# A gated attention and long-convolution kernel on one core: 24 places of its stored task order changed, and its last tenth put in a new order

## The chip, the cores and the metric

The kernel runs on one core of a Trainium2 chip. The core has five engines with a queue of instructions each: TensorE (PE in the profile; its weight loads are listed apart as PEld), VectorE (DVE), ScalarE (ACT), GpSimd (POOL) and SyncE (SP), and 16 DMA engines that they share. The metric is the device time of one execution in microseconds; the median of several runs is compared.

## The reference

B = 8 batches, S = 3136 positions, D = 256 channels, 64 channels for the scores; everything comes in and goes out in f32.

```python
scores = np.matmul(z, z.transpose(0, 2, 1)) / S
attn = np.maximum(scores, 0.0) ** 2
x = u * np.matmul(attn, v)
proj = x @ w_proj                      # 256 -> 768
x1, x2, x3 = proj[..., :D], proj[..., D:2*D], proj[..., 2*D:]
X2 = np.fft.rfft(x2, n=S, axis=1)
H = np.fft.rfft(filter_fft, n=S, axis=0)[None]
conv = np.fft.irfft(X2 * H, n=S, axis=1)
out = (x1 * conv * x3) @ w_out
```

The scores are symmetric, since both sides are z.

## The kernel before, in words

**The stages of a batch.** The 3136 positions of a batch are cut into seven chunks (five of 512, one of 256, one of 320). Attention goes by units, pairs of 128-row tiles against a chunk: PE multiplies z with z into a PSUM pair, ACT or DVE takes the relu of it (L1956 on ACT, L1958 on DVE, into a tile R_t of which there are 3), ACT or DVE squares it (L1965, L1967, into A_t, of which there are 8), and PE weighs v with it. Because the scores are symmetric, a squared tile also serves the mirrored unit, after a DMA transpose on SP's queue (L1885, into M_t, M2e_t or M2o_t by chunk). DVE multiplies the sum with u into xT_t (L2012). For a chunk PE then makes the projection; ACT or DVE evicts one gate factor (x_t), DVE makes the gate product (gate_t, L1293).

**The convolution** is an FFT of 3136 = 64 x 49 written as matmuls with two round trips over DRAM. The first transform is evicted to s_t and put to DRAM (L1065, L1068), and loaded back with the other index on the partitions (L1099; for the last batch L1114, into spec_in_t and gs_t). PE transforms again ("quads"), evicts to xh and R_t (L619, ACT's copies; L623, DVE's), DVE multiplies with the filter's spectrum (L1394, L1398, L1399), PE transforms back, the result is evicted (in the last batch into M_t, M2e_t, M2o_t, A_t and uT_t, which are free by then), put to DRAM (L1443) and loaded again (L1128, into conv_in_t, v_t or A_t). PE makes the last step, DVE multiplies with the gate into yT_t (L1499), PE applies w_out, ACT or DVE evicts (ost_t; for the last batches also v_t, R_t, xh, gs_t) and the rows are stored (L1548).

**Who loads and stores.** POOL issues the loads of u, v and z (L662, L688) behind small copies that wait for a task (L673, L676), and casts z and v at the start. SP issues mirrors, the turns of z and u (L1657, L1602), puts, loads and most stores, strictly in its own order: an instruction that waits holds up those behind it. In the last 50 us some ends of batches 5 and 6 are left over for PE to work on during the last batch's round trips, and batch 6's stores go by POOL's queue.

**What sets the order.** All this is some 5,400 tasks. A class Plan holds them with the engines that each may run on and what each waits for. Its function go walks four tables at the head of the file. ORDER (L50) names the tasks two characters at a time, for all engines in one sequence, in which each engine's instructions are issued; ENGINES (L163) says for each task that could go to either ACT ("a") or DVE ("d") which one takes it; BANKS (L180) names the PSUM pair for each task of PE that takes one; CODES is the alphabet. An entry of ORDER past the last task is a filler: eight matmul instructions with an identity that no one reads (in the profile ps_s<-ident). The times the class works with are its own; nothing but these tables decides the order.

Of the kernel before, what the change touches and what calls it, by code (L numbers as in the profile page):

```python
# [2106 lines left out]
```

## Time and profile before

| | |
|---|---|
| runs | 941.12, 946.83, 946.80 us; median 946.8 |
| the profiled execution | 942.77 us, of which its span 940.9; granted clock 0.997 |
| PE, DVE, ACT, POOL busy | 914.0, 838.7, 819.6, 247.6 us |
| matmuls | 12425 |
| DMA moved | 170.70 MB, mean 181 GB/s |
| the chain that ended last | 83% of it on PE, 5% each on ACT, DVE and DMA |

The page gives busy times and, further down, groups of instructions by source line. A row of a timeline has the start in us, the length, the engine, the line, the operation with its tiles and how many, and in brackets how long the engine was idle before and what it is thought to have waited for. A row of the chain of waits has start, length and the engine with the tile. A row of the windows has, for a stretch of time, the busy time of PE, weight loads, DVE, ACT and POOL with the number of instructions, then PE's granted clock, the busy share of the DMA engines and the GB/s they moved. Several instructions of one kind in a row stand in one row.

### The profile page before, as it was taken

What the parts mean: (1) busy time and instruction counts of PE and PEld (TensorE: products, weight loads), DVE (VectorE), ACT (ScalarE), POOL (GpSimd) and SP (SyncE); (2) the same over time, 40 slices, a digit from 0 to 9 for tenths busy, and PEclk for the clock granted to TensorE, in tenths of its full rate; (3) what the DMA queues carried; (4) which work ended last, traced back from release to release, by engine and by line L of the source; (5) the groups of instructions that cost most, each with busy time, mean ns of one, the idle gap of its engine ahead of it and who ended that gap; (6) DMA issues with size and microseconds to landing.
All of it is one profiled execution on the core that took longest, in us unless ns stands there. A gap on an engine that the chain in (4) does not pass through costs nothing.

```text
span 940.9 us, 30306 instructions
## 1 busy us (share of the span) xinstructions
PE 914.0 (97%) x12425; PEld 555.4 (59%) x12425; DVE 838.7 (89%) x1117; ACT 819.6 (87%) x952; POOL 247.6 (26%) x585
## 2 busy tenths in 40 slices
PE   8999999999999999999999999999999999999985
PEld 3445655566554666556565565666565666676654
DVE  8886899999888998999889988999988999899795
ACT  7877898999889998898989999899988999899673
POOL 5143322332332312223122231333123141101030
PEclk9999999999999999999999999999999999999999
DMA  9899899989999789998999989998999979898867
GB/s 158 155 176 163 141 156 197 185 144 173 169 218 201 151 190 168 206 200 146 192 173 212 177 160 189 178 223 149 200 167 208 224 128 202 202 205 140 207 193 232
DMA packets 331644, 170.70 MB, mean 181 GB/s; under 512 B 242887, under 2 KB 307143, under 8 KB 331505
## 3 DMA queue, kind: packets, MB, share of 16 engines
q1 hardware_dynamic: 301624, 131.98, 70.2%
q0 software_dynamic: 29168, 35.13, 25.8%
q8 instruction: 97, 1.59, 0.7%
q10 hardware_dynamic: 712, 1.66, 0.6%
q14 instruction: 43, 0.34, 0.2%
HBM read 90.26 MB, written 53.05 MB: 152 GB/s over the span
## 4 chain that ended last, share of the span: by engine, by line
PE 83%; ACT 5%; DMA 5%; DVE 5%; issue 2%; SPq 0%; POOL 0%; DVEq 0%; ACTq 0%; POOLq 0%
PE ps_s L553 82%; DMA M_t<-A_t 3%; ACT R_t L1956 2%; DVE xh L1394 1%; DVE A_t L1967 1%; DMA zn_t<-in_z_dram 1%; ACT A_t L1965 1%; DVE xT_t L2012 1%; DMA A_t<-spec 0%; ACT xh L619 0%; DMA spec<-uT_t 0%; ACT ost_t L619 0%; ACT s_t L619 0%; DVE gs_t L623 0%; ACT R_t L619 0%
## 5 line engine op out<-in xcount | busy, mean ns | idle before, releaser
L553 PE MATMUL ps_s<-A_t,v_t 64*128 64x512 bf16 (+5 forms) x4766 | 515.7, 352 | 1.1 <-DVE A_t L1967 1.0
L553 PEld LDWEIGHTS <-v_t 64*128 64x128 bf16 (+1 forms) x6528 | 305.8, 98 | 185.9 <-PE ps_s L553 19.2
L1956 ACT ACTIVATE R_t<-ps_s 128x1024 f32<-128x1024 f32 (+3 forms) x359 | 336.8, 961 | 50.4 <-PE ps_s L553 47.2
L1965 ACT ACTIVATE A_t<-R_t 128x1024 bf16<-128x1024 f32 (+2 forms) x281 | 271.8, 992 | 12.0 <-DVE R_t L1958 4.9
L1967 DVE SCALAR_TENSOR_TENSOR A_t<-R_t 128x1024 bf16<-128x1024 f32 (+3 forms) x211 | 233.6, 1123 | 17.6 <-ACT R_t L1956 10.3
L553 PE MATMUL ps_s<-zT_t 64*128 64x512 bf16 (+5 forms) x1186 | 191.4, 352 | 4.4 <-DVE gate_t L1293 1.7
L1958 DVE TENSOR_SCALAR R_t<-ps_s 128x1024 f32<-128x1024 f32 (+4 forms) x153 | 170.3, 1124 | 23.7 <-PE ps_s L553 13.3
L676 POOL COPY tick<-A_t 1x1 bf16<-1x1 bf16 x159 | 54.3, 341 | 426.0 <-ACT A_t L1965 262.0
L553 PE MATMUL ps_s<-xT_t,wp 64*128 64x512 bf16 (+3 forms) x976 | 124.3, 352 | 0.5 <-DVE R_t L1958 0.4
L553 PEld LDWEIGHTS <-zT_t 64*128 64x128 bf16 (+1 forms) x1219 | 68.9, 97 | 52.8 <-issue 9.8
L553 PE MATMUL ps_s<-M_t,v_t 64*128 64x512 bf16 (+4 forms) x860 | 96.6, 353 | 1.8 <-DMA M_t<-A_t 1.7
L619 ACT ACTIVATE x_t<-ps_s 128x1024 bf16<-128x1024 f32 (+3 forms) x75 | 69.4, 927 | 20.9 <-PE ps_s L553 18.1
L1394 DVE TENSOR_TENSOR xh<-xh,H 128x1024 bf16<-128x1024 bf16 x120 | 81.8, 685 | 2.9 <-ACT xh L619 2.0
L1293 DVE TENSOR_TENSOR gate_t<-ps_s,x_t 128x512 bf16<-128x512 f32 (+2 forms) x112 | 64.5, 617 | 12.4 <-PE ps_s L553 10.3
L2012 DVE TENSOR_TENSOR xT_t<-ps_s,uT_t 128x512 bf16<-128x512 f32 (+2 forms) x112 | 64.0, 614 | 6.5 <-PE ps_s L553 6.1
L1499 DVE TENSOR_TENSOR yT_t<-ps_s,gate_t 128x1024 bf16<-128x1024 f32 (+2 forms) x53 | 56.9, 1078 | 12.9 <-PE ps_s L553 11.7
L553 PEld LDWEIGHTS <-wp 64*128 64x128 bf16 (+1 forms) x976 | 47.8, 96 | 30.0 <-PE ps_s L553 2.0
L553 PE MATMUL ps_s<-wp,xT_t 64*128 64x256 bf16 (+2 forms) x944 | 64.0, 266 | 0.1
L553 PE MATMUL ps_s<-wo,yT_t 64*128 64x256 bf16 (+2 forms) x904 | 62.3, 266 | 1.0 <-DVE yT_t L1499 0.5
L662 POOL DMA_DIRECT2D un_t<-in_u_dram x112 | 58.1, 519 | 18.5 <-issue 16.0
L688 POOL DMA_DIRECT2D v_t<-in_v_dram x112 | 58.4, 525 | 13.6 <-issue 10.3
L553 PEld LDWEIGHTS <-xT_t 64*128 64x128 bf16 (+1 forms) x944 | 43.5, 97 | 19.1 <-issue 0.6
(157 smaller groups left out, 910.2 us busy)
## 6 DMA issues: line engine op xcount, KB each, us to landing
out_dram<-ost_t SPq DMA_DIRECT2D x60, 256.0 KB
spec_in_t<-spec SPq DMA_DIRECT2D x56, 192.0 KB
spec<-gs_t SPq DMA_DIRECT2D x56, 192.0 KB
v_t<-in_v_dram POOLq DMA_DIRECT2D x80, 128.0 KB, 4.5
un_t<-in_u_dram POOLq DMA_DIRECT2D x80, 128.0 KB, 4.5
spec<-s_t SPq DMA_DIRECT2D x40, 256.0 KB
conv_in_t<-spec SPq DMA_DIRECT2D x34, 256.0 KB
out_dram<-ost_t SPq DMA_DIRECT2D x18, 128.0 KB
```

The source lines that it names most:

```text
L553: got = nc.tensor.matmul(o, *args, **kw)
L619: got = nc.scalar.activation(out_, in_, AF.Copy)
L662: nc.gpsimd.dma_start(out=t[ds(j * N1, N1), lo - t0 : hi - t0, :], in_=x[:, n2 : n2 + hi - lo, :])
L688: nc.gpsimd.dma_start(out=t[ds(j * N1, N1), ds(v_at(a), (b - a) * D)], in_=r[:, n2 + a - lo : n2 + b - lo, :].rearrange("p t d -> p (t d)"),)
L1293: has_read(nc.vector.tensor_tensor(o[:, :, ::-1] if h == 0 else o, p, x, ALU.mult), p)
L1394: nc.vector.tensor_tensor(x[:, 1 - i], x[:, 0], h, ALU.mult)
L1499: has_read(nc.vector.tensor_tensor(yb["y"][:, :, 0:w], p, gates[b, c][:, :, 0:w], ALU.mult), p)
L1956: has_read(nc.scalar.activation(r, p, AF.Relu), p)
L1958: has_read(nc.vector.tensor_single_scalar(r, p, 0.0, ALU.max), p)
L1965: nc.scalar.activation(a, r, AF.Square, scale=1.0 / float(S))
L1967: nc.vector.scalar_tensor_tensor(a, r, inv_s2, r, ALU.mult, ALU.mult)
L2012: has_read(nc.vector.tensor_tensor(x[:, :, ::-1] if h == 0 else x, f, ut, ALU.mult), f)
```

## The change

Only the tables change; the tasks and what they compute are the same. ORDER had 13 fillers and has 7. Some 30 tasks change between ACT and DVE, three of them before 850 us: one relu of the first batch goes from DVE to ACT, and two squares. ACT has 955 activations instead of 951. Named by the times of the profile before, the places up to 850 us are:

- 29: a relu moves to ACT and PE takes its neighbours in another order; 64 to 72: POOL's casts ahead of a filter load; 66 to 71, 85, 91, 119: PE swaps neighbouring matmuls
- 164: SP's turn of u later; 270 to 311: SP's mirrors earlier, stores and a spectrum put later
- 375: a square on ACT one place earlier; 393 (to 409) a store later, 484 a turn of u later, 541 (to 552) and 618 (to 628) stores later, all on SP
- 491, 599, 618: PE swaps neighbours; 607: a square to ACT; 839 to 850: a turn of u and a square on ACT earlier

From about 852 us on the whole of the rest is new. The diff is three long tables; its first line that differs, and one of ENGINES:

```diff
 ORDER = (
...
-    "1S1P1a1c110M1Xr!1d1U1g0N1b1Er#1h1k1Y1er$1l1o1J1ir%1f1p1m1s1j1=1tr&1qr(1>1]1n1u1}1^22r)231r1?1v271_r*"
+    "1S1P1a1c110M1Xr!1d1U1g1E0N1br#1h1k1Y1er$1l1o1ir%1f1J1p1m1s1j1=1tr&1qr(1>1]1n1u1}1^22r)231r1?1v271_r*"
...
 ENGINES = (
...
-    "aaaaaaaadaaaaaadaaaadadaad"
+    "aaaaaadadaadaaadaaaadaddad"
```

**SP, around 270 to 291 us.** SP's queue; the rows are mirrors (M2e_t, M2o_t, M_t, out of A_t), turns of z and u, spectrum loads and output stores (out_dram). Before:

```order
L1099 DMA spec_in_t<-spec_1_60 48x2048 x2
L1099 DMA spec_in_t<-spec_1_60 2x2048
L1885 DMA_TRANSPOSE M2e_t<-A_t 128x8x128
L1657 DMA_TRANSPOSE zT_t<-zd_t 128x8x128
L1602 DMA_TRANSPOSE uT_t<-un_t 128x8x128
L1548 DMA out_dram<-ost_t 64x1024 x4
L1099 DMA spec_in_t<-spec_1_60 48x2048 x2
L1099 DMA spec_in_t<-spec_1_60 2x2048
L1885 DMA_TRANSPOSE M2o_t<-A_t 128x8x128
L1885 DMA_TRANSPOSE M_t<-A_t 128x8x128 x2
L1443 DMA spec_1_62<-gs_t 48x2048 x2
```

Now:

```order
L1885 DMA_TRANSPOSE M2e_t<-A_t 128x8x128
L1099 DMA spec_in_t<-spec_1_60 48x2048 x2
L1099 DMA spec_in_t<-spec_1_60 2x2048
L1657 DMA_TRANSPOSE zT_t<-zd_t 128x8x128
L1602 DMA_TRANSPOSE uT_t<-un_t 128x8x128
L1548 DMA out_dram<-ost_t 64x1024 x2
L1099 DMA spec_in_t<-spec_1_60 48x2048 x2
L1099 DMA spec_in_t<-spec_1_60 2x2048
L1885 DMA_TRANSPOSE M2o_t<-A_t 128x8x128
L1885 DMA_TRANSPOSE M_t<-A_t 128x8x128 x2
L1548 DMA out_dram<-ost_t 64x1024 x2
```

The M2e_t mirror is now ahead of a load, and two of the four stores stand behind the M2o_t and M_t mirrors.

**POOL, the end of its queue.** v_t, ost_t, R_t and xh hold finished rows; ost_t and v_t are batch 6's, R_t and xh the last batch's. Before:

```order
L1443 DMA spec_1_62<-A_t 2x1024
L1443 DMA spec_1_62<-uT_t 2x1024
L1548 DMA out_dram<-v_t 64x512 x2
L1548 DMA out_dram<-v_t 64x768
L1548 DMA out_dram<-v_t 64x512
L1548 DMA out_dram<-ost_t 64x1024 x2
L1548 DMA out_dram<-R_t 64x1024
L1548 DMA out_dram<-xh_118 64x1024
```

Now:

```order
L1443 DMA spec_1_62<-uT_t 2x1024
L1548 DMA out_dram<-v_t 64x1024 x2
L1548 DMA out_dram<-v_t 64x512 x2
L1548 DMA out_dram<-R_t 64x1024
L1548 DMA out_dram<-ost_t 64x1024 x2
L1548 DMA out_dram<-xh_118 64x1024
L1548 DMA out_dram<-v_t 64x768
L1548 DMA out_dram<-v_t 64x512
L1548 DMA out_dram<-ost_t 64x1024 x2
```

Three of batch 6's stores (ost_t twice, the 64x768 and 64x512 rows of v_t) now stand behind the last batch's R_t, two of them behind its xh as well; the store of a v_t pair that went earlier now stands just behind the puts.

**ACT, in the last spectrum (898 to 912 us).** Evictions of the last batch's spectrum; ost_t is an output of batch 6. Before:

```order
L619 ACTIVATE R_t<-ps_s_139 128x512
L619 ACTIVATE ost_t<-ps_s_140 128x1024
L619 ACTIVATE M_t<-ps_s_141 128x512 x2
L619 ACTIVATE M2e_t<-ps_s_140 128x512
L619 ACTIVATE R_t<-ps_s_139 128x512
```

Now, the last evictions of it and what follows:

```order
L619 ACTIVATE M2o_t<-ps_s_141 128x512 x2
L619 ACTIVATE A_t<-ps_s_139 128x512
L619 ACTIVATE uT_t<-ps_s_140 128x512
L619 ACTIVATE v_t<-ps_s_142 128x512
L619 ACTIVATE x_t<-ps_s_141 128x1024
L619 ACTIVATE ost_t<-ps_s_139 128x1024
```

The ost_t eviction has moved behind the spectrum's evictions and the gate factor x_t that follows them.

More of the change, by code (lines that the diff above doesn't have):

```diff
@@ new lines @@
+    "r}r~2e3Y2f363ks03i3Z3l2g2u372h2w3as13r3B3ss23vs33w2p3b2i2q3c3m2js42k3t3d3n3e3x3f3C2l0c2v0es50d3Q3Ss6"
+    "0f3$0g3D3%3)s73os83*3ys93&3R3;3p3j3<3q3+3u3#3!3=3(3:3z3E3,493F4G4AsAsB3/4H3>0lsC4B4IsD0msE0nsF4J4K4N"
+    "4C4O0osG4R3-4D4S3?4E3G4TsH4P444X4UsI4Y3H3T4F3I4b3U454L4csJ4M4Z4W4i4d4msK4n4j0p4e4V3.0q4Q0r4o4a4f4vsL"
+    "4k0ssM4p4h4w4g3J4l4x3K3@4s3L3V4q4?sN46sO4@3[sP3]4t50sQ514u4[4y52573^584]sR474^0t0usS530v3_4z4_4{594|"
+    "0w4}5D3{4r5M4:5EsT4;4~5NsUsV5FsW565O5h555A5l5i5s5B5C5m5GsX545JsY5t5wsZ5j5L5#3M5n5K5P5x3N5usa5o5$sb5y"
@@ new lines @@
+    "5H3O5k5)5q5*sc5Q5-3P5%5r5.3|4<5e5&5v5f4=5+3}5(5z3~5<sd485=5I4!se5/5!5>4#sf4$5?5^5p0x0y5,5_5@0z5}sg5:"
+    "5;5{5~5]0!7n7r607osh7vsi7ssjsk7w4%7psl5|5[7t4&7x7z61404(7!sm41sn427%627q7&7u7#437k7)7lso7*7.7(4)7y7/"
+    "7$7?7+4*7@sp4>4+7_7,7-7{7:5R7~5Ssq5T7[sr7;7<807>7|847]0#ss85815U0$5V7^5W0%88827}86st898D8a0&su8E8b83"
+    "7=8f8Asv8F878c8m8Bsw8n8C8g8Gsx8o0(8q8h8d0)sy0*8e8r8i0+sz8j0,8xs!8H8ys#8#8k8s8$8V8l8W0;4,638zs$4-648t"
+    "4.8p8%8u8+s%654/8:8w8,8&8;8v5X8(s&5Y8-665Z5g8[s(8)8<8]8!8|s)8}8^8=9K8*9L8>8/8~9S8.679T8@0-689Ms*0.0/"
@@ new lines @@
+    "8_0<s+0=s,0:5a8{5b8I8X5c0>909U0?5d690@8J9V9Y8K6A9Zs-7m9Ws.0{9N6B9a9O9b91s/8Y9c9P9i9Q9j9F9d9n8?9Gs:9t"
+    "9o9R9u9y9k9e9X9f8L9ps;9z6C8M9v9h9q8N9r6D0[6Es<9w9m9!0]9)A1s=9*A29s9#9$6F0^s>9+0_0|9xs?9g0}0~8O109(A3"
+    "9l8P928Q8ZAB9Hs@A46GA59,ACAF93AGs[AD6TAMs]94s^AH8RANs_9I8SA69-8TAIAQs{A7AR9{958U9|98AOAS9&96A8AX97A9"
+    "AJAY9%99ATs|AU9AAb9J6HAcAA6I9.AZs}AjAE6JAk6M9/6K6jAL6N6LA)AP9:A*s~6RAd6Ot09BAl6SA:AKAe9CAWAft1A;6P6U"
+    "AVt26Q6VAa9Dt3A+Ah6ZA[t46W6at59}9;6XA]Ai6b6c6Y9<6dAm9=6ht6A<t76eA,6iA=A{AnA>A-6zA|A.A^6k6fB2A#A/A$6g"
@@ new lines @@
+    "B69E6lt89~B7t9B36pA?6m6qA@AgA}tAB4BD6nA~9>B06otBBE6r9?B8tCA09@BHA_BFB9BIBQBAB5tDBRB1BJBCBlBvBGA%BmBB"
+    "BwBK6sBLBP6t6x9[A&6ytEBS9]tF6u9^BNB!AoB#tGBntH9_BT6vBxB)BOApBo6wtIB*BqAqB$tJBMB<tKBrB=BUBsB%BtB&C8tL"
+    "C9tM6!B>BiB+BuBj6#BzB,B(CAB-CCtNCJCD6$6(BytO6)CKB;Ar6%tPB/CE6+As6&6,tQCFBpAtAuCLCNtRB:AvCO6-6:AwB?6."
+    "CB6*tS6;6/CSCHtTB@CT6<CPCICUC5B.A(Ax6=CVCXCWAyCYCMAztUC6CbCQ6>CZCgCRChCnCctVCoCaBVCiA!CdCrtWCpEECsCj"
+    "BWCkCeEFBXtXCGBYCfCtEIEGBZEJtYEMCmBaENCqCu6?BbEK6}tZEOtaBcEQClBkB[BdtbERtcB]tdB^teESEUEXEVEHELCvEPEY"
@@ new lines @@
+    "Gut+Fx7NGSt,GTGDGv7OG&GJG(GCGO7PFyGwt-GZG+Fz7cG)GxG<GyC,GWF!t.G=Gat/G,G>GV7QG@7RF-G[t:C^7SGzG-t;F#Gb"
+    "G]G}G.G!G/F.F$G~G^G#GpF/G_G$F%GqGcH0H2GdH3t<GUGeC-G%C.H4t=7LHAC<HBt>C/G*DAH5t?C=C:H6HXC;t@HYC_C>G;C{"
+    "G?C?HeC[H8C@HCt[C]G|HfD0G:t]C|H1D1D3Grt^G{D4C}HlF&C~t_Hm7VF(D57T7WH9F)7XGfHDD6HZ7YD7HpGgHgHnD2t{7Zt|"
+    "HqHht}GhHi7aHaHrHvt~HEHwHsDQHzHbHcH!HxHSGiHTF*HFH#GsH)GjHdH*GtH$HGH%H7u0GkHHH-u1HtH.D8H+HjD9H@HkH[Hu"
+    "DBH/Hou2DCICH]DGH=H:u3H;u4DHIDu5DJH&HyDKDD7dH(HUDEIE7eHVH,7fGlIMu6INDFGmIRH?GnDLu7ISH^IOGou8IXIHH<DM"
@@ new lines @@
+    "ufD$L)LaL*ugD<L-IrL#uhL.DqLxIsL$LyLbL%ItL&I!L>IuuiL+L?LpL]LqIvL(IwL/ujL^JNIxL,M0L@L:JOL_ukDvJPulM1L{"
+    "L;DwL<M5L|umDxM6L=MCunM2MDJQJTM7JRL}L[JSJUD%M8JVK)MEM9M3MHL~MID&LrM4MFD(MJD+JWMBMGMKLsD,JXLcD-JYuoLd"
+    "D_LfLeJZupLgMeDyLhuqMfMmurusMnutD)D=MgMLLiD>MhMoLjMAD?MZMsMaMiMtMjLkMvMkMwE3LtMpMMMuMqM$MNJaM%LlMxuu"
+    "uvMOM*LmuwMyM+JnLnMluxM,M:D.M;M&uyM-M?M.M!MrM<M}M@M#MzM)M~M(D/M[NLD:M/NVuzMbNMM]M>NWu!N0NZu#NNNgMPNa"
+    "M=u$NXMQNONhM^u%LoNPD@MRNbM{JbD[JcNcM|D]MSD;u&NiJdJgN1MTJeJhu(J%JfMdNQMUJoN2u)JpNRNkM_Jiu*NGNlNHNrJq"
@@ new lines @@
+    "JlJjNSNsMcMVJkNTNdNUNtJmJtMWu+JuJru,NvJsMXu-NYNmNeNwJwJ#NfJxNjJ$NnNoN%u.N&JvNqNxN3J&u/JyJ(NyNzN}N(Np"
+    "N4N~NuJzu:N5O5J!N$O6OCJ@J)u;D{O0N)ODu<OGO7J*D|u=MYD}O1N#OHu>O8J+O9OMN6N*ONO2D^N7OEu?NIN]u@N8N^OIJ,NJ"
+    "OQJ-O3OOD~O4OJORE0N!OAOKE1J/OBOSJ:E4J>J.u[J?E5J;J[OTu]OUE6J]u^OXOLJ<u_OYK0J=OFK1J^ObOVOkOcu{OZOPN9J_"
+    "OlE2O(OWJ{NAO)K2u|NKO<u}OdNBN+OaOmK3OhOeOjOfNCK4O=N,OnN_OiO*N-O-u~NDv0O+O>N{NEO[v1O.O]O/OoN.v2v3NFO:"
+    "O^O}O$v4OgO%P7O~N/P8O;P0O_PSO{v5N:PTO@P1PWO?O|P9v6PUE7PXP4PdP6E8PeN;PYv7P5PfE9PhPAPZO,N<PiPmv8EAN=N|"
@@ new lines @@
+    "TNKiKXS;T8TFT9S9KwKjTATLT0TGT1SAQ1vlTOSBTTTYTBSKTHTZKfTCTUTPvmvnTaTISCS<TVSDTbTSS%TcSETeTQS=TfvoS>vp"
+    "TjTgS?TkSFTXS@TRTrTlS[T;vqTdTsTmTiT<TnTWvrTtTqT2T{U0Q2T|U1vsT=vtQ3KkT}TuT>QET?KlQ4Q7KmvuQ8vvThKpU7vw"
+    "Q5U8KqT@TvT[U9QUUBvxKrT,T]UCT-Q6S]T^Q9S^UDTpU2vyT4T_S_UEUIUFQAUMvzUJT3U3QBS{U4T~UNS|UKQCv!S}QFv#QGTo"
+    "QDU6UUv$UVQKQHKnTwUAQLQIKsTxQJS~UOKtQNTyUHU5KuULUPUQUWv%QOUrv&UsT.UyUGQSQPUTUzKxv(QQQTUXQRKyTzUtKzQV"
+    "QMT!v)QWT#U(v*U)v+QkQXT$U!QaUYT%UuQbT:U#UvQYU$T/UZT&QZUmUwUnQdUaU*QeUSv,UbUxU,QfU<URU-v-QgU@U=U%QhU&"
@@ new lines @@
+    "YRQ)Q@YawHVSQ/YTYWYdQ*YeQ:YbQ+YXwIQ;Q,YYYiwJQ~YjYfYmV+Q-wKYnV,YkYcYhYgYoYrV-Y;wLY<YswMYlY@Y=YqYtY}Yp"
+    "Q<wNY[Q=YuY~Q>YSV.wOY]V/Z2V:V[wPZ0Y>Z3Y^Q?Y_Y?Y{YvZ9Y|ZAQ[wQZ4Q]Y,ZDZBY-R7V;wRV<Q^wSZEwTZ5Z1V=Z6Z7ZF"
+    "Z8ZKZCZLWhV>ZGWnZHWiZIWoZMWjWkwUWpWlZPWmX}ZJZQwVZWYwZXZRZbZNZOZcwWY.ZSZTQ_ZYYxY/Q{ZyYyQ|wXZZwYZVZzZd"
+    "Z)WqwZZ*Q}WrZ/WsZaZ!ZeZ+Z#WtZ:Z<Z$waZ=Z,Z;Z%Z-wbZUZ>wcZfZ&Z^wdZ?Z_Z~ZtZ(Zua0wea5Z{aAa6YzZ@wfa1aBwgY!"
+    "Z[R0aCa2Y#Z.a3Z]aIZ|Z}aDa7aJR1afaEwhR2a4aKa8a9apagaHaqatwiaLauaha!aGR3wjara#aiR4ajR8wkRFR5ZvwlR9a&av"
@@ new lines @@
+    "RARNwmaka(WuwnawalaMa$Y$a.woW*a/Y%aaabwpY&ama)Zwa<ana=a_Y(aoa{aFa:Y)bIwqY*a|Zgwra>bJY:axZhwsa*a+ZiY+"
+    "bPasbQa?ayZja@bKZmZkazZlbWwtbXZna,WvZoZxbRa%wuWwacbSW!bTa-W#RBWxadwvbaWya;bbWzRCW_W+W$RDZpa^W,Zqa}Zr"
+    "bga]wwW%W(bhW&aNwxbYW)bLR6aObiW-bMbNbcaPa[W:wyW.bdwzW;beW/W=w!a~W>bOZsbkw#REblW?W]bDbUbEaQW^W@RGbVW<"
+    "W[bmRHaRRIW{w$aSW|bnbZbobrw%XBbsW}bvX1w&W~bww(X0b&btbfbjX2bqb(X4bubxRJX5w)bpb|RKb)w*b}bybzX9w+X3RLX6"
+    "w,XAb~c7b%cCb*c8b#c2X7c0c3cDw-X8cIw.b$cJbFw/w:b+c9c4c5cRaTcEb!cKw;b^cmb_w<cSaUcncFcLc6aeaVcAcBcTcHcq"
@@ L156 @@
[L156 to L160 removed]
+    "Xacffqcgfzfuf&chXbd8f+f#f:Xdcid9f;Xef,dAxIf-XsxJXff?dEf@f(dFf<xKdGf|f!dBf}f/dCXgf[dDerg2f.Xhg3f~f>f]"
@@ new lines @@
+    "f^XlxLXifcgPf=xMg4f{XmgXgQX!xNgYxOfdxPXng1gZgddHxQgRgeg0gadIfNgbg5dJfOgfXodKfPxRXpxSf_XqgSg6gggTghgU"
+    "XjgngKxTgLgogsXtgVXrgtXuxUXvX#gixVX+gygpgWgzgjgkX$xWguX=fQX%gcdLg%gvfRgwg!g&fTxXgmfSg(glg.fUg/grg)fV"
+    "fexYg*gqh6gxh7XwfWg$g:fXh8g-XxgMfYg7h9hAxZXyg8dYhGxag9hHxbhKg#g;hLhIhRgAxchSfZgBgNhVhMgCxdgDhWxehNhT"
+    "hOgEg,dMgFgOg<hBhCdNg+hchDhdh1hXdRh2xfhEdSdOgGdZgHXzhYdPdaxghZdQhghFgIdodThJhQdbhhxhdUhohexidVg=h/hp"
+    "dcgJxjddhUh:hPhiX&g>hqh@X(g?hahjh[xkhkxlh;X)hbX,dWh]h3hmX-xmX.h}dXhfh^h~h_hndeh4g@dfhri2g[i0hli3xng]"
@@ L192 @@
+    "210231023102132012032131201201320321032130130212031203"
 )
```

177 lines of the change are left out of this document (60 added, 117 removed).

## The prediction

> **What bounds the kernel now.** I read the page's busy times and its row of slices first, then the share of the chain by engine, then what PE waits for, then the chain of waits near the end.
>
> ```profile
> span 940.9 us, 30306 instructions
> PE 914.0 (97%) x12425; PEld 555.4 (59%) x12425; DVE 838.7 (89%) x1117; ACT 819.6 (87%) x952; POOL 247.6 (26%) x585
> PE   8999999999999999999999999999999999999985
> PE 83%; ACT 5%; DMA 5%; DVE 5%; issue 2%; SPq 0%; POOL 0%; DVEq 0%; ACTq 0%; POOLq 0%
> 853.16 32.27 PE ps_s L553 x543
> ```
>
> PE is busy for 914.0 of 940.9 us, and 83% of the chain is PE. The last row, from the chain of waits of the last 91 us, is one unbroken piece of PE work of 32.27 us in 543 matmuls. So a new order can win only where PE waits, or at the end, where PE has run dry: 940.9 less 914.0 leaves 26.9 us for everything together. Of the new order's last tenth the first 32 us (853 to 885) are full: what ACT, DVE and the queues do in another order there is hidden by PE, and I count it at nothing.
>
> Outside the end, these are PE's waits near which something is moved (the timeline of PE: start, length, then in brackets the idle time before and its releaser):
>
> ```profile
> 30.38 0.61 PE L553 MATMUL ps_s<-xT_t,wp 64*128 64x512 bf16 x4 [0.37 <-DVE R_t L1958]
> 79.92 0.60 PE L553 MATMUL ps_s<-M_t,v_t 64*128 64x512 bf16 x4 [0.91 <-DMA M_t<-A_t]
> 295.31 0.39 PE L553 MATMUL ps_s<-zT_t 64*128 64x512 bf16 x2 [1.69 <-DVE gate_t L1293]
> 390.76 0.41 PE L553 MATMUL ps_s<-spec_in_t,S 49*64 49x512 bf16 x4 [1.68 <-ACT xh L619]
> ```
>
> **The change, part by part.** The first 850 us hold some 24 small moves; each is weighed by the wait that stands beside it.
>
> The wait at 30.38 is for a relu on DVE. That relu goes to ACT, and PE takes its neighbours in another order: -0.4.
>
> The wait at 295.31 is the largest whose cause is moved. DVE (first row) waits 1.78 us before it can write a square. The row names ACT as releaser, but what comes free is a buffer of the pool A, and the last reader of that buffer is the mirror transpose M_t<-A_t on SP's queue. The SP rows show a queue without a gap, in which the mirrors stand behind four output stores and three loads:
>
> ```profile
> 292.84 1.23 DVE L1967 SCALAR_TENSOR_TENSOR A_t<-R_t 128x1024 bf16<-128x1024 f32 x1 [1.78 <-ACT ost_t L619]
> 279.67 3.55 SPq L1548 DMA_DIRECT2D out_dram<-ost_t  x4
> 283.32 3.10 SPq L1099 DMA_DIRECT2D spec_in_t<-spec  x3
> 286.52 1.27 SPq L1885 DMA_TRANSPOSE M2o_t<-A_t  x1
> 287.90 2.65 SPq L1885 DMA_TRANSPOSE M_t<-A_t  x2
> ```
>
> The change puts two of the four stores behind the mirrors. Half of 3.55 us is 1.8 us, which covers the 1.78 us of DVE, and so the 1.69 us of PE: -1.7. Bounds: 0, if the transfers and not the issue set the transposes' end, and -1.7. I take the full value, because the queue is continuous and the shift is as long as the wait. Late next are the two stores, which nobody on PE waits for, and a spectrum put behind them.
>
> The waits at 79.92 and 390.76 have an edit beside them (GpSimd casts in another order at 64 to 72; one square on ACT a place earlier at 375), but neither edit touches the mirror's DMA or the xh eviction that the rows name. Count 0, bound -2.6 (0.91 + 1.68). The other moves (stores and transposes of u moved along SP's queue at 164, 393, 484, 541 and 618, swaps of neighbouring matmuls, the square at 607) stand where PE has no gap over 0.9 us. Count 0; bounds: +0.9, one mirror late as at 79.92, and nothing to gain.
>
> Between 885 and 898 the kernel is on a round trip over DRAM: SP puts the last part of the first transform and loads it back, and the spectrum's matmuls begin.
>
> ```profile
> 880.00:890.00 10.00, 9.75 (x144) 6.08 (x142) 6.31 (x10) 3.98 (x5) 0.00 (x0) 1.00 0.82 237
> 889.99 0.36 SPq L1065 DMA_DIRECT2D spec<-s_t  x1
> 894.38 1.68 SPq L1114 DMA_DIRECT2D spec_in_t<-spec  x4
> 897.24 1.15 PE L553 MATMUL ps_s<-spec_in_t,S 49*64 49x256 bf16 x11
> ```
>
> (The first row is of the windows: span; busy PE, PEld, DVE, ACT, POOL; clock; DMA share; GB/s.) The put's issue, the loads 4.4 us later and the first matmul 2.9 us after them stay as they are. But a batch-5 output store that was issued about 20 us earlier now stands ahead of the put. Bounds: 0, and 328 KB at 237 GB/s = +1.4. I take 0: the store's tile is long ready, the put waits for its own eviction, and earlier store traffic also leaves its place.
>
> From 900 to 912 the last spectrum's evictions fill ACT and DVE.
>
> ```profile
> 900.00:905.00 5.00, 4.40 (x89) 2.68 (x81) 5.00 (x9) 5.00 (x11) 0.58 (x2) 1.00 0.23 75
> 905.00:910.00 5.00, 3.66 (x80) 2.17 (x78) 5.00 (x9) 5.00 (x12) 2.13 (x4) 1.00 0.86 202
> 903.00 1.13 ACT ost_t L619
> 904.13 0.74 ACT M_t L619 x2
> 910.96 0.76 DVE L1499 TENSOR_TENSOR yT_t<-ps_s,gate_t 128x640 bf16<-128x640 f32 x1
> 911.77 0.69 DVE L623 CAST uT_t<-ps_s 128x512 bf16<-128x512 f32 x1
> 913.70 3.91 DMA spec<-uT_t
> 919.02 4.18 DMA A_t<-spec
> ```
>
> Both windows read 5.00 of 5.00 for ACT and DVE. The change takes one output eviction out of ACT's part (903.00; it holds the chain for up to 1.13 us; the evictions behind overlap, so by their starts about 0.9) and one gate product out of DVE's (910.96 to 911.77, 0.8). Three spectrum evictions go from ACT to DVE and three back. So the last put starts 0.8 us earlier, and with it the store of 3.91 and the load of 4.18 us. Bounds: 0 and -0.9.
>
> Behind the load PE multiplies, and the outputs run out:
>
> ```profile
> 920.00:925.00 5.00, 3.66 (x84) 2.85 (x86) 2.94 (x3) 0.80 (x2) 1.03 (x2) 1.00 0.88 263
> 925.00:930.00 5.00, 4.71 (x100) 3.54 (x97) 3.87 (x7) 3.14 (x7) 1.06 (x2) 1.00 0.94 285
> 930.00:935.00 5.00, 3.21 (x62) 2.05 (x56) 4.08 (x8) 2.51 (x6) 0.00 (x0) 1.00 0.86 270
> 935.00:941.00 6.00, 0.00 (x0) 0.00 (x0) 0.12 (x1) 0.00 (x0) 0.00 (x0) 0.78 0.61 175
> 923.25 0.40 PE L553 MATMUL ps_s<-T,A_t 64*128 64x128 bf16 x8 [0.61 <-DMA A_t<-spec]
> 928.45 0.82 DVE x_t L623
> 904.42 1.06 POOL L1548 DMA_DIRECT2D out_dram<-ost_t  x2 [5.42 <-ACT ost_t L619]
> 913.52 2.13 POOL L1548 DMA_DIRECT2D out_dram<-v_t  x4
> 920.00 1.03 POOL L1548 DMA_DIRECT2D out_dram<-ost_t  x2 [4.35 <-ACT ost_t L619]
> 926.17 0.54 POOL L1548 DMA_DIRECT2D out_dram<-R_t  x1 [5.14 <-ACT R_t L619]
> ```
>
> The gate eviction x_t (928.45, on the chain) goes from DVE to ACT: -0.8. The store at 920.00 no longer goes beside the load that PE waits for at 923.25: -0.4 of the 0.61. With the 0.8 above, the last products are ready 2.0 us earlier.
>
> Against this stand the stores. Three of POOL's stores of batch 6 (904.42: 524 KB; the second half of 913.52: 328 KB; 920.00: 524 KB, together 1.38 MB) now queue behind batch 7's first halves, the first of which is at 926.17. DMA from 925 on is already at shares of .94, .86 and .61, and the kernel ends with its last byte, not with PE, which has nothing in the last window. The store at 920.00 lay partly in this stretch already, so I take half of it and the other two whole: 1.1 MB more. At 285/.94 = 303 GB/s they take 3.7 us. The idle DMA time that they may fill is 5 x (.06 + .14) + 6 x .39 = 3.3 us; I take half, 1.7, since the last window tapers off behind the last products. The stretch begins 1.2 us earlier (0.8 by the put, 0.4 by the load; the x_t eviction lies inside it and moves no byte). 3.7 - 1.7 - 1.2 = **+0.8**. Bounds: -2.0 (all hidden, the products' earlier end counts) and 1.38 MB at 270 GB/s = +5.1.
>
> The DMA page of the Trainium skill, "DMA: Bandwidth & Descriptors", section "Queues, rings and completion order", says that a DMA engine takes turns between its queues packet by packet; by that POOL's late stores share the engines with SP's instead of going behind them, which leaves the sum of bytes, and so this term, as it is. No row here separates the two.
>
> The order also drops 6 of 13 filler products. Nothing waits for them; what cover they gave is the clock, below.
>
> **Sum:** -0.4 - 1.7 + 0.8 = -1.3 us, all other terms nought. Against the profiled execution of 942.77 us (1.9 more than its span) that is 941.5. The runs shown are 941.12, 946.83 and 946.80, median 946.8; with the profiled one, the middle of four is (942.77 + 946.80)/2 = 944.8. I set the sum against that: **943.5 us**.
>
> **Rivals.**
>
> A, faster: the late stores drain in idle DMA time and the front's uncounted waits go too. -0.4 - 1.7 - 2.0 - 2.6 = -6.7, 938 us. For it: 3.3 us of idle DMA share from 925 on, and edits stand beside the waits. Against: the shares of .94 and .86.
>
> B, slower: the stores become the end. 1.38 MB at 270 GB/s is 5.1 us without cover, the batch-5 store ahead of the put adds 1.4, and the front's -2.1 stays: +4.4, 949 us (951 if the front gives nothing). It decides once the late stores are more than the earlier start and the idle share can take: (1.2 + 3.3) us x 303 GB/s = 1.36 MB if every idle moment is filled, (1.2 + 1.7) x 303 = 0.88 MB if half. For it: the end is DMA. Against: those stores are ready long before 926, and their queue need not wait for it.
>
> C, the clock: the fillers keep PE from idling.
>
> ```profile
> 914.63 1.24 PE L553 MATMUL ps_s<-ident 64*128 64x512 bf16 x10
> 918.48 1.03 PE L553 MATMUL ps_s<-ident 64*128 64x512 bf16 x8
> 920.72 0.40 PE L553 MATMUL ps_s<-T,A_t 64*128 64x128 bf16 x8 [1.22 <-DMA A_t<-spec]
> ```
>
> The rows count matmuls by form and hold filler products; the granted clock is 1.00 in the windows above up to 935, with idle times up to 1.22 us beside them. If those at 918.48 are among the six that go, the idle time there is about 1.03 + 1.22 = 2.3 us. Should the clock halve there, 3.66 us of PE work (920 to 925) would double, less the 1.34 us idle in that window: +2.3, from which with the sum's -1.3 comes 945.8. "TensorE: Matmul & The Clock Gate" of the Trainium skill, in Part 1 on the clock gate, gives an activity window of about 3.4 us; by that 2.3 us would not be enough, and the rows up to 1.22 us agree as far as they go.
>
> D: the waits only move to neighbours: no change, 944.8.
>
> **How the numbers follow.** Forecast 0.50 (own range 940 to 947), A 0.27, B 0.13, C 0.05, D 0.05. About 1% (9.4 us) is what a measurement of this kernel can tell from no change, since its own runs lie 5.7 us apart. None of the cases passes it by its own number; with a spread of that size a little under half of A's 0.27 does, 0.12 for faster, and over half of B's 0.13, 0.08 for slower; the rest is 0.80. The range reaches from A's 938 less 2 (a fast run of it) to the upper end of B: 936 to 951.
>
> **What would show it.** In the changed profile: the gap of 1.69 us at 295 and that of 0.37 at 30.4 gone, PE's total idle time before 850 about 2 us less; the last spec put some 0.8 us earlier against the start of the spectrum; PE's last matmul about 4 us earlier (0.4 + 1.7 + 2.0), and the DMA shares of the last 15 us nearer to 1 with a taper that is shorter. It is wrong if the DVE wait near 293 stays, if the put near 890 is late, if PE's clock falls below 1.00 in the end, or if PE in the new last tenth waits between 853 and 885, where I count nothing.

## The result, and the profile after

The change makes the kernel slower: 954.29 us in the median of 6 runs (953.0 to 961.77) against 945.86 for before (941.12 to 950.74), a ratio of 1.0126 with a 95% interval of 1.0091 to 1.0162. The ratios here and below are taken over undisturbed runs alone, which leaves out among others one of before at 3354 us and the profiled one of e8_mended at 1354 us, and are not the quotients of the medians (1.0089 here). The profiled execution took 954.52 us. Rows of the page:

```profile
span 952.7 us, 30191 instructions
PE 912.8 (96%) x12367; PEld 554.1 (58%) x12367; DVE 833.4 (87%) x1113; ACT 823.0 (86%) x956; POOL 245.1 (26%) x585
PE   8997999999999999999999999999999999999974
PE 78%; DVE 7%; DMA 7%; ACT 4%; issue 2%; POOL 0%; DVEq 0%; SPq 0%; POOLq 0%; ACTq 0%
```

and one of the chain of waits:

```profile
859.79 33.80 PE ps_s L553 x535
```

PE works as long as before; the fourth slice, about 71 to 95 us, has fallen from 9 to 7. The unbroken piece of PE work in the new last tenth is there again (33.80 us). PE's waits, in the timeline of PE:

```profile
29.23 0.39 PE L553 MATMUL ps_s<-zT_t 64*128 64x512 bf16 x2 [1.48 <-ACT R_t L1956]
84.73 1.04 PE L553 MATMUL ps_s<-M_t,v_t 64*128 64x512 bf16 x4 [6.42 <-DMA M_t<-A_t]
297.44 0.39 PE L553 MATMUL ps_s<-wo,yT_t 64*128 64x256 bf16 x4 [0.65 <-DVE yT_t L1499]
655.46 0.31 PE L553 MATMUL ps_s<-zT_t 64*128 64x320 bf16 x2 [1.03 <-DVE xT_t L2012]
928.14 0.40 PE L553 MATMUL ps_s<-T,A_t 64*128 64x128 bf16 x8 [2.02 <-DMA A_t<-spec]
```

The wait for a mirror that was 0.91 us (at 79.92) is 6.42 us. What the clock does behind it stands in the windows:

```profile
76.00:80.00 4.00, 2.32 (x21) 1.00 (x17) 3.65 (x6) 0.91 (x3) 0.18 (x2) 1.00 1.50 96
80.00:84.00 4.00, 0.00 (x0) 0.00 (x0) 0.00 (x0) 0.78 (x1) 1.72 (x4) 0.57 1.37 121
84.00:88.00 4.00, 3.27 (x20) 1.27 (x22) 1.22 (x1) 1.68 (x2) 0.00 (x0) 0.58 1.16 144
```

The granted clock falls to 0.57, and the four products with M_t behind the wait take 1.04 us where they took 0.60. The end, in the windows:

```profile
930.00:935.00 5.00, 5.00 (x108) 4.08 (x103) 4.78 (x7) 2.35 (x5) 1.90 (x4) 1.00 0.48 120
935.00:940.00 5.00, 4.65 (x93) 3.35 (x90) 4.37 (x8) 3.12 (x8) 2.23 (x5) 1.00 0.95 296
940.00:945.00 5.00, 0.27 (x4) 0.00 (x0) 0.76 (x2) 0.66 (x3) 0.00 (x0) 0.91 1.01 327
945.00:952.70 7.70, 0.00 (x0) 0.00 (x0) 0.00 (x0) 0.00 (x0) 0.00 (x0) 0.50 0.50 165
```

and in POOL's timeline:

```profile
920.16 2.11 POOL L1548 DMA_DIRECT2D out_dram<-v_t  x4
933.10 0.52 POOL L1548 DMA_DIRECT2D out_dram<-R_t  x1 [10.82 <-ACT R_t L619]
933.62 1.04 POOL L1548 DMA_DIRECT2D out_dram<-ost_t  x2
934.64 0.52 POOL L1548 DMA_DIRECT2D out_dram<-xh  x1
935.15 1.05 POOL L1548 DMA_DIRECT2D out_dram<-v_t  x2
936.20 1.03 POOL L1548 DMA_DIRECT2D out_dram<-ost_t  x2
```

POOL stands for 10.82 us at its queue's head, R_t, with batch 6's rows behind it. The last of those rows are evicted by 927.2 us (ACT ost_t, DVE v_t). The DMA engines are half idle from 930 to 935 (0.48, 120 GB/s), and full with 327 GB/s when PE has ended.

**Where the time went.** The span is 11.8 us longer. I compared the start of each task on PE in the two traces, took the median by stretch (the "shift"), and beside it the end of the last DMA packet; the time from PE's last matmul to that packet is called the drain. Before 64 us the change is 0.7 us ahead; at 85 us it is 6.1 behind; at 840 it is 7.7 behind; PE's last matmul ends 6.4 later (940.3 against 933.9) and the last packet lands 11.3 later (950.5 against 939.2). So 6.8 us come from one place at 64 to 85, 1.6 from all places between, and 3.6 from the new last tenth, in which PE gains and the drain grows from 5.3 to 10.2 us.

### The profile page after: what moved, and what is told of

It is laid out like the page before. It is cut to its first block, busy times and chain, and to the rows that moved or that the text cites. A ratio compares the mean times of both kernels' runs of the same rounds, so it can differ in the third digit from the quotient of the medians.

```text
span 952.7 us, 30191 instructions
## 1 busy us (share of the span) xinstructions
PE 912.8 (96%) x12367; PEld 554.1 (58%) x12367; DVE 833.4 (87%) x1113; ACT 823.0 (86%) x956; POOL 245.1 (26%) x585
## 4 chain that ended last, share of the span: by engine, by line
PE 78%; DVE 7%; DMA 7%; ACT 4%; issue 2%; POOL 0%; DVEq 0%; SPq 0%; POOLq 0%; ACTq 0%
PE ps_s L553 78%; DMA M_t<-A_t 3%; DVE xh L1394 2%; DMA M2e_t<-A_t 2%; ACT R_t L1956 1%; ACT A_t L1965 1%; DVE xh L623 1%; DVE A_t L1967 1%; DVE R_t L1394 1%; DVE yT_t L1499 0%; ACT gs_t L619 0%; DVE xT_t L2012 0%; DMA A_t<-spec 0%; DVE R_t L1958 0%; DMA spec<-uT_t 0%
## 5 line engine op out<-in xcount | busy, mean ns | idle before, releaser
L1956 ACT ACTIVATE R_t<-ps_s 128x1024 f32<-128x1024 f32 (+4 forms) x363 | 339.2, 959 | 52.2 <-PE ps_s L553 42.7
L1965 ACT ACTIVATE A_t<-R_t 128x1024 bf16<-128x1024 f32 (+2 forms) x284 | 274.9, 994 | 17.6 <-DMA M_t<-A_t 7.5
L1967 DVE SCALAR_TENSOR_TENSOR A_t<-R_t 128x1024 bf16<-128x1024 f32 (+4 forms) x208 | 229.3, 1118 | 27.2 <-ACT R_t L1956 11.9
L1958 DVE TENSOR_SCALAR R_t<-ps_s 128x1024 f32<-128x1024 f32 (+2 forms) x149 | 166.7, 1131 | 24.3 <-PE ps_s L553 13.6
L553 PE MATMUL ps_s<-wo,yT_t 64*128 64x256 bf16 (+3 forms) x888 | 61.4, 266 | 1.2 <-DVE yT_t L1499 0.6
L673 POOL COPY tick<-xT_t 1x1 bf16<-1x1 bf16 x54 | 10.5, 195 | 184.9 <-DVE xT_t L2012 184.6
```

The lines of the kernel that those rows point to most:

```text
L553: got = nc.tensor.matmul(o, *args, **kw)
L1956: has_read(nc.scalar.activation(r, p, AF.Relu), p)
L1958: has_read(nc.vector.tensor_single_scalar(r, p, 0.0, ALU.max), p)
L1965: nc.scalar.activation(a, r, AF.Square, scale=1.0 / float(S))
L1967: nc.vector.scalar_tensor_tensor(a, r, inv_s2, r, ALU.mult, ALU.mult)
```

## The experiments

The theories are named in the texts of what was expected. Each kernel was timed beside the kernel before on the same chip. The runs of before in these series reach from 936 to 957 us but for the one named above, so a time alone resolves some 0.3 to 0.4%; smaller pieces are read from the traces, of which there is one for each kernel.

**Front and end apart.** The first kernel has all edits up to 850 us and the old order behind, the second the reverse.

```diff
 e1_front: ORDER up to 850 us of the change + ORDER from there of before
 e2_tail:  ORDER up to 850 us of before + ORDER from there of the change
```

> All the small edits up to 850 us, with the old order from there on. The traces of before and after, laid side by side on PE, are 7.9 us apart at 850 us. Theory 1 (the front loses by itself, nearly all of it at 64 to 85 us; the end loses apart from it): 6 to 9 us slower than before. Rival 2 (the loss belongs to the new last tenth alone): within 2 us of before.

> The old order up to 850 us, the new last tenth behind it. Theory 1: PE's last product comes about 2 us earlier and the stores drain 5 to 6 us longer, so 3 to 4.5 us slower than before, with some 11 us between PE's last matmul and the last DMA packet instead of 5.3. Rival 2 (late stores are only the echo of a late front): no longer drain, 2 us faster than before.

e1_front: 952.84 us against 943.76, ratio 1.0128 (1.0071 to 1.0185). e2_tail: 944.27, ratio 0.9999 (0.9972 to 1.0025). The front loses by itself, so rival 2 falls. In time the new last tenth shows no loss, where 3 to 4.5 us were expected, though in its trace the drain is 10.1 us, as expected; more on that below.

**The load order at 64 to 70 us.** Theory 1 named POOL's order; the experiments changed it alone in before, and put it back in the change.

```diff
 POOL (e3_pool_alone; e4_pool_undone is the change with the reverse)
+L662 DMA zn_t<-in_z_dram, L688 DMA v_t<-in_v_dram
+L676 COPY tick<-A_t
 L762 DMA xh<-in_moe_filter_fft_dram
-L662 DMA zn_t<-in_z_dram, L688 DMA v_t<-in_v_dram
```

> Before, with one thing changed: at 64 to 70 us POOL issues the z and v loads ahead of the filter load, as in the change. Theory 1 (the filter load then lands in the middle of SP's mirror transposes, and both slow down): a PE wait of 5 to 6.5 us near 79 for M_t, 5.5 to 7 us slower than before, with PE's clock below 1.00 there. Rival 1 (another edit before 80 us, the relu at 29 or the swaps of PE, sets the wait): wait near 79 stays at 0.9 us, time within 1 us.

> The change with that one POOL order put back. Theory 1: the PE wait near 79 is 1 us again and the time 5.5 to 7 us below the change, that is 1 to 4 us above before. Rival 1: as the change, within 1 us.

e3_pool_alone: 942.46 us, ratio 1.0012 (0.9983 to 1.0041): no loss, and theory 1 falls as it stood. e4_pool_undone: 948.38, ratio 1.0036 (1.0007 to 1.0066), with no PE wait near 79: so the order does matter in the change. Something else must be needed beside it. The SP and POOL timelines of before:

```profile
68.52 4.31 SPq L1885 DMA_TRANSPOSE M_t<-A_t  x2
...
64.88 1.23 POOL L762 DMA_DIRECT2D xh<-in_moe_filter_fft_dram  x2 [0.29 <-issue]
```

e3_pool_alone's PE, SP and POOL timelines:

```profile
80.65 0.60 PE L553 MATMUL ps_s<-M_t,v_t 64*128 64x512 bf16 x4 [1.82 <-DMA M_t<-A_t]
...
68.34 6.66 SPq L1885 DMA_TRANSPOSE M_t<-A_t  x2
...
66.83 1.23 POOL L762 DMA_DIRECT2D xh<-in_moe_filter_fft_dram  x2
```

and the same of the change:

```profile
66.97 7.42 SPq L1885 DMA_TRANSPOSE M_t<-A_t  x2
...
66.31 1.23 POOL L762 DMA_DIRECT2D xh<-in_moe_filter_fft_dram  x2
```

In the change the transposes are issued 1.4 us sooner, 0.7 us behind the filter load; in e3_pool_alone 1.5 us behind it, in before 3.6. PE's part of the same place is the reason: PE weighs v with the old M_t tiles ahead of two products with A_t, and the mirrors' buffers come free sooner. That was theory 3, and I tried the halves on before:

```diff
 PE (e5_pe_alone; e6_both_halves has POOL's order from above too)
+L553 MATMUL ps_s<-M_t,v_t (x4)
 L553 MATMUL ps_s<-A_t,v_t (x4)
-L553 MATMUL ps_s<-M_t,v_t (x4)
```

> Before, with only PE's half of the change at 66 to 71 us: PE weighs with the old mirrors M_t ahead of two products with A_t, so the mirrors' buffers come free earlier. Theory 3 (the two halves collide: PE's half starts SP's M_t transposes about 1.1 us earlier, POOL's half sends the filter load 2 us later, and only with both do they start together): transposes begin near 67.2 us, no PE wait over 1 us near 79, 0 to 1.5 us faster than before. Rival 4 (PE's half alone makes the wait, since M_t is then needed earlier): a wait of 3 us or more.

> Before, with both halves of that one place. Theory 3: the wait of 4 to 6.5 us for M_t near 79 to 85, a transpose packet of 256 bytes at about 51 ns instead of 33, and 6 to 10 us slower than before: the whole of the change's loss from one place. Rival 4b (the other 17 places in front have a share in it): under 3 us slower.

e5_pe_alone: 943.52 us against 945.76, ratio 0.9968 (0.9933 to 1.0002). e6_both_halves: 947.17, ratio 1.0034 (1.0001 to 1.0066). The waits, from PE's and SP's timelines of e5_pe_alone:

```profile
79.80 0.61 PE L553 MATMUL ps_s<-M_t,v_t 64*128 64x512 bf16 x4 [1.18 <-DMA M_t<-A_t]
...
67.26 5.35 SPq L1885 DMA_TRANSPOSE M_t<-A_t  x2
```

and of e6_both_halves:

```profile
82.93 0.61 PE L553 MATMUL ps_s<-M_t,v_t 64*128 64x512 bf16 x4 [4.30 <-DMA M_t<-A_t]
...
67.27 7.63 SPq L1885 DMA_TRANSPOSE M_t<-A_t  x2
```

In its window behind the wait the clock (0.58) is halved too:

```profile
84.00:88.00 4.00, 4.00 (x22) 1.34 (x18) 1.34 (x2) 2.95 (x3) 1.64 (x4) 0.58 1.32 172
```

Neither half makes the wait (1.82 and 1.18; without either 0.91 in before and 1.78 in e2_tail); both together do (4.30; in the kernels with all of the front 4.07, 6.42 and 7.00). In these four the transposes are issued 0.6 to 0.7 us behind the filter load, in e5_pe_alone 2.8. The filter load's time from issue to landing tells the same, in the DMA views of before, e3_pool_alone, e6_both_halves and the change:

```profile
xh<-in_moe_filter_fft_dram POOLq DMA_DIRECT2D x2, 256.0 KB, 5.6
```
```profile
xh<-in_moe_filter_fft_dram POOLq DMA_DIRECT2D x2, 256.0 KB, 7.1
```
```profile
xh<-in_moe_filter_fft_dram POOLq DMA_DIRECT2D x2, 256.0 KB, 8.6
```
```profile
xh<-in_moe_filter_fft_dram POOLq DMA_DIRECT2D x2, 256.0 KB, 8.4
```

The transposes' packets of 256 bytes that start between 64 and 86 us take 33 ns in the mean in before, 32 in e3_pool_alone and 31 in e5_pe_alone, but 51 in e6_both_halves and 53 in the change. The loads that stand behind the filter's in POOL's queue slow down too (that of w_out from 5.6 us to 11.5 and 13.5), so which of POOL's loads meets the transposes isn't separated. Theory 3 holds for the wait. In time it was expected to cost 6 to 10 us and measured 3.2 (0.1 to 6.2), next to rival 4b's under 3; PE's shift in the trace goes from -0.4 to +4.7, that is 5.1 us, 3.4 of them the longer wait and the rest the halved clock. That it is the whole of the front's loss this run doesn't show: e1_front lost 12 us by its ratio (6.7 to 17.5). Whether the other edits in front lengthen the wait (4.07, 6.42 and 7.00 us with them, 4.30 without) stays open; without the pair they cost nothing that can be measured, as the last two runs show.

**The stores at the end.** The change with batch 6's three stores ahead of the last batch's:

```diff
 POOL (e7_stores_first)
+L1548 DMA out_dram<-ost_t, v_t, ost_t  (batch 6)
 L1548 DMA out_dram<-R_t
-L1548 DMA out_dram<-ost_t  (batch 6)
 L1548 DMA out_dram<-xh
-L1548 DMA out_dram<-v_t, ost_t  (batch 6)
```

> The change with one thing put back at the end: on POOL the three stores of batch 6 stand ahead of the last batch's two. Theory (the queue's head waits until 933 for R_t while finished rows stand behind it): PE's last matmul to the last DMA packet falls from 10.2 us to 6 to 7, time 3 to 4 us below the change; the front's wait stays. Rival (the new order makes those rows too late anyway, or their bytes only move ahead into the load that PE waits for): within 1 us of the change.

950.03 us, ratio to before 1.0045 (1.0000 to 1.0089): below the change by 4.3 us in the medians and by 0.8% in the ratios, where 3 to 4 us were expected. In its windows the DMA engines no longer idle ahead of PE's end, and in POOL's timeline, below them, the first of the stores are issued 7 us ahead of R_t:

```profile
930.00:935.00 5.00, 3.96 (x86) 2.90 (x82) 3.58 (x3) 1.34 (x3) 2.03 (x4) 1.00 1.01 308
935.00:940.00 5.00, 4.85 (x106) 3.87 (x104) 4.71 (x10) 3.03 (x6) 1.05 (x2) 1.00 1.02 362
945.00:949.70 4.70, 0.00 (x0) 0.00 (x0) 0.00 (x0) 0.00 (x0) 0.00 (x0) 0.67 0.55 188
```

```profile
928.95 1.03 POOL L1548 DMA_DIRECT2D out_dram<-ost_t  x2 [4.91 <-ACT ost_t L619]
935.63 0.53 POOL L1548 DMA_DIRECT2D out_dram<-R_t  x1 [3.60 <-ACT R_t L619]
```

The drain behind PE's last matmul is 5.3 us again. The reverse, before with the late stores and nothing else, and the new last tenth with early stores behind the old front:

```diff
 e11_late_stores_alone: before, POOL's last five stores in the order of the change
 e10_tail_stores_first: e2_tail with the edit of e7_stores_first
```

> Before, with one thing changed: POOL's three stores of batch 6 put behind the last batch's, as the change has them, nothing else of the new last tenth. If POOL's queue order is the cause of the longer drain: 9 to 10 us from PE's last matmul to the last packet, 3 to 5 us slower; the load that PE waits for near 923 may land 0.4 us sooner. If the cause is the later evictions of those rows: under 2 us slower.

> The old order up to 850 us, the new last tenth, its stores put first on POOL. If the late stores are what spoils the new last tenth: 5.3 us between PE's last matmul and the last packet instead of the 10.1 of the run with the new last tenth alone, and 1 to 4 us faster than before. If the gain of the mended kernel came from its two edits in front: no faster than before.

e11_late_stores_alone: 946.03 us against 942.4, ratio 1.0025 (0.9998 to 1.0051), drain 8.7 us: the drain grows nearly as expected, the time by 2.4 us, between the two forecasts (3 to 5, and under 2). In its windows PE has ended and the stores run on at full rate:

```profile
930.00:935.00 5.00, 2.34 (x40) 1.54 (x40) 2.77 (x6) 1.51 (x4) 0.00 (x0) 0.97 1.02 327
935.00:940.00 5.00, 0.00 (x0) 0.00 (x0) 0.00 (x0) 0.00 (x0) 0.00 (x0) 0.50 0.95 327
```

e10_tail_stores_first: 944.4, ratio 1.0012 (0.9983 to 1.0041), drain 5.2 us: no gain in time, where 1 to 4 us were expected. From the traces, the stretch from 840 us to the last packet can be taken by itself (the shift of the last packet less PE's shift at 840, both against the profile of before):

| last tenth | profiles | stretch | drain |
|---|---|---|---|
| old | before, e1, e5, e6, e12, e3 | 0, +1.0, +3.8, -0.1, -0.1, +3.2; mean +1.3 | 5.2 to 5.4 us |
| old, stores late | e11 | +5.0 | 8.7 |
| new | the change, e2, e4 | +3.6, +3.1, +5.4; mean +4.0 | 9.8 to 10.2 |
| new, stores early | e7, e9, e10, e13, e14 | -0.5, -1.3, -1.0, -2.0, -0.1; mean -1.0 | 5.2 to 5.9 |

By these means the late stores cost about 5 us (4.0 + 1.0), and the rest of the new last tenth wins about 2 against the old one's mean. In sum the new last tenth is +2.7 in the mean of few profiles with a spread of 3, near what e2_tail's interval allows (up to +2.4). But part of the spread is PE's clock. In seven of these profiles, old order and new (e1, e3, e5, e11; e2, e4, e10), the granted clock falls to 0.50 for 3.4 to 13.7 us somewhere between 897 and 921 us, in the others not. A window of e4_pool_undone:

```profile
902.00:906.00 4.00, 3.78 (x58) 2.91 (x51) 3.03 (x6) 4.00 (x9) 0.00 (x0) 0.50 0.04 16
```

Without these seven the old order is at 0, -0.1 and -0.1, the new one at +3.6, and with early stores at -0.5, -1.3, -2.0 and -0.1: the late stores still cost 4 to 5 us, but the rest of the new last tenth wins about 1. The times say less. Between kernels that differ in the late stores alone, the ratios differ by 0.8% (the change and e7), 0.5% (e4 and e13), 0.25% (e11 and before) and -0.1% (e2 and e10): three point to a cost, one to none, and its size of 4 to 5 us is shown by the traces alone.

**A kernel from the parts that looked good**, measured twice: before's front with the relu on ACT and PE's half at 66 to 71 us, then the new last tenth with the stores early.

```diff
 e8_mended = e9_mended_again: e10_tail_stores_first
+ the relu at 29 us on ACT; PE's half of the place at 66 to 71 us
```

> Before up to 850 us with two edits of the change, the relu on ACT at 29 and PE's half at 66 to 71, then the new last tenth with the stores put first as in the run with the stores put back. If the three readings hold, -1 from the front, -1 to -2 from PE's end and 0 to +2 from the stores: 0 to 3 us faster than before. Rival (the new last tenth costs something else): 2 us slower or more.

> The same kernel as the mended one, with more rounds and a profile that can be read. By theory no PE wait over 1 us near 79, about 5.3 us from PE's last matmul to the last DMA packet, 2 to 5 us faster than before. If the first result was luck: within 1.5 us of before.

The first time 940.29 us, ratio 0.9957 (0.9928 to 0.9986); the second 941.63, ratio 0.9996 (0.9969 to 1.0024). The gain did not come again, and this kernel isn't shown to beat the one before.

**The edit at 618 us.** PE projects a chunk before it scores the next unit.

```diff
 PE (e12_618_alone)
+L553 MATMUL ps_s<-wp,xT_t
 L553 MATMUL ps_s<-zT_t ...
-L553 MATMUL ps_s<-wp,xT_t
```

> Before, with only the edit at 618 to 628 us (PE projects a chunk before it scores the next unit, the gate factor's eviction earlier on DVE, one store later on SP). In all four profiles with the front's edits PE waits 0.5 to 1.3 us for xT_t near 650, in none of five without. Theory: that wait appears, some 1 us, and the time stays within what the rounds can tell. Rival (the wait needs other edits): no wait near 650.

943.21 us, ratio 1.0007 (0.9979 to 1.0035). The wait is there; the timeline of PE:

```profile
648.67 0.61 PE L553 MATMUL ps_s<-M2o_t,v_t 64*128 64x256 bf16 x8 [0.57 <-ACT gs_t L619]
653.13 0.31 PE L553 MATMUL ps_s<-zT_t 64*128 64x320 bf16 x2 [1.13 <-DVE xT_t L2012]
```

Its shift grows by 2.1 us between 640 and 651; the time can't tell it.

**Both orders put back.** Still open was whether a third cause of their size exists.

```diff
 e13_two_undone:   the change with POOL's orders at 64 to 70 us and at the end of before's kind (e4 and e7)
 e14_three_undone: the same, and the edit at 618 us undone
```

> The change with two POOL orders put back, the loads at 64 to 70 us and the stores at the end; its other places and the rest of its new last tenth stay. If these two are the whole loss but for the edit at 618: no PE wait over 1.5 us near 79, 5.3 us from PE's last matmul to the last packet, and between 1 us faster and 3 us slower than before, against 12 slower for the change. If a third cause of their size exists: 5 us slower or more.

> The same with the edit at 618 to 628 us undone as well. The wait near 650 goes, 1 to 2 us below the run before it on this list; within 2 us of the kernel before the change. If the wait near 650 was hidden elsewhere: the same time as that run.

e13_two_undone: 941.9 us against 941.12, ratio 0.9985 (0.9952 to 1.0018). e14_three_undone: 942.32, ratio 1.0001 (0.9965 to 1.0037). With the two orders of POOL put back the change no longer loses; all its other places together make no difference that can be measured. e14_three_undone has no wait near 650, but the time shows no gain from that.

## Why the prediction was wrong

The forecast was -1.3 us and a range of 936 to 951; it came out 8.4 us slower by the medians. Step by step:

- **The wait at 79.92** is the step that failed. I counted the loads at 64 to 72 at nothing, with a bound of a gain only, because "neither edit touches the mirror's DMA". It does: the load order sends 256 KB pieces of the filter into the time in which the transposes run, and PE's swap at 66 to 71, which I had put down as a swap of neighbours (count 0, bound +0.9), makes the transposes start sooner. Measured: 6.8 us in the change's trace (5.5 of wait, 1.3 of clock). I weighed the two halves one by one; their cost is in the pair, which e3, e5 and e6 show.
- **The stores** were seen, and their bytes (1.38 MB), but the size was off: +0.8 with an earlier start of 1.2 and 1.7 us of idle time filled. The traces show +4 to +5 for the stores and -1 to -2 for the rest of the new last tenth. The idle time could not be filled, as those rows, evicted by 927, stood in POOL's queue behind R_t until 933; they came in one piece behind it. At the 327 GB/s of the last window 1.38 MB take 4.2 us. Rival B had this mechanism at +5.1 for the stores, and called it against the odds because the rows are ready long before 926; ready rows don't help behind a head that waits. Its +1.4 for the put near 890 isn't seen: from 885 to 900 PE's shift grows by over 1 us in one of eight profiles with the new last tenth (e4, 1.5) and in three with the old one (e1, e5 and e11, 1.3 to 4.2).
- **The wait at 295** (-1.7): the wait for gate_t is smaller with the edited SP order (0 in the change, and 1.39, 2.63, 0.90, 0 and 0 us in the other profiles that have it; in nine with the old order 0 to 2.37, in the mean 1.70), but other waits near it grow (for yT_t up to 1.61), and PE isn't further on: from 260 to 340 us its shift grows by 1.3 us in the mean of the six, and by 1.0 in that of the nine (-1.4 to +4.3). So the term isn't seen. The mirrors do start 1.8 us sooner in the mean, as forecast, but the row of the two M_t mirrors lasts 3.9 to 5.7 us with the edit, where it lasts 2.6 to 4.4 without; in the change:

```profile
292.42 4.20 SPq L1885 DMA_TRANSPOSE M_t<-A_t  x2
```

  That is the bound of 0 that I had named: the issue of the mirrors does not set their end alone.
- **The relu at 29** (-0.4): the 0.37 us wait is gone, but the one ahead of it went from 1.12 to 1.48, so PE's idle time there is the same. Yet PE's shift falls by 0.3 us between 28 and 32 us in each of the seven profiles with the edit, and by 0.05 at most in the others: the term was about right, though not by the wait that I counted.
- **PE's chain to the end** (-2.0): from 840 us to its last matmul PE wins 1.3 us in the change, 1.6 in e2_tail and 0.3 to 2.1 in the five with early stores, and loses 0.9 in e4: mostly a gain, smaller than I put it.
- **853 to 885 counted at nothing:** right; 33.80 us unbroken. A wait of 1.09 us stands just ahead of it at 858.7.
- **The other moves counted at nothing:** the one at 618 makes a wait of 0.5 to 1.3 us in each of the five profiles that have it beside other edits and 1.13 in the one alone, and from 640 to 651 PE's shift grows by 0.7 to 2.1 us in these six and by nothing in the rest: mostly over the bound of 0.9.
- **The clock (rival C)** fell in the change at another place: not where the fillers went, but around the wait at 79, for 6.8 us from 80.6 on, 2.2 us into the wait. The Trainium skill, "TensorE: Matmul & The Clock Gate", Part 1, gives an idle window of about 3.4 us before the clock halves. The waits of 6.42 and 4.30 us, both with a granted clock of 0.58 behind them, are longer than that, though in the change the clock fell before 3.4 us of the wait had passed; others are shorter. In e5_pe_alone one wait of 2.35 us (at 297.84) and in e12_618_alone one of 2.98 us (at 394.14) have a halved clock behind them, too:

```profile
298.00:302.00 4.00, 4.00 (x30) 2.39 (x28) 2.12 (x3) 2.36 (x3) 2.91 (x7) 0.57 1.17 257
394.00:398.00 4.00, 3.86 (x40) 1.95 (x40) 2.71 (x5) 2.94 (x4) 0.00 (x0) 0.50 0.97 231
```

  So the 2.3 us of the rival could have been enough. A length that decides doesn't come out of these profiles: in the last tenth the clock fell with no single wait over 2.25 us, and a wait of 2.63 us in e4 (at 296.37) left it at 1.00. It fell there in four profiles with the old last tenth and three with the new, so no effect of the fewer fillers is seen.

## What to carry to other kernels

Judge moved transfers by what is on the DMA engines at the same time, not only by what they wait for: two moves that each do nothing can meet. In an in-order queue, ask what stands at the head: ready stores behind a late one can cost their whole length at the end. And a wait of 1 to 2 us seen in one profile can be absent in the next of the same order, or come back as another wait when it is removed; read several, and see whether PE is further on behind it, before you count its removal. Look at the clock, too, before you put a difference between two profiles down to their order.
